# Branch arm widths of the expert products taken from a table by expert

## The chip, the cores and the metric

The kernel runs on one core of one Trainium2 chip. The metric is the device time of one execution in microseconds (us); less is better. The core has five engines that run side by side and wait for each other by semaphores: PE (TensorE, the matrix products), DVE (VectorE), ACT (ScalarE), POOL (GpSimd) and SP (SyncE, which here issues nearly all DMAs). In the profile the weight loads of PE have a row of their own, PEld. An engine's name with a q behind it (PEldq) is its sequencer, which issues the instructions, takes the branches and waits for semaphores.

## What is computed

Three layers follow one another: clustered attention, a mixture of experts with one expert per token, and a gated feed-forward layer. Only the middle one is touched:

```python
def _moe_ref(x, w_gate, w1, w2, capacity):      # x: 1536 tokens x 512; 8 experts, F = 1024, capacity 384
    logits = x @ w_gate
    expert_idx = np.argmax(logits, axis=1)
    ...                                          # gate_w, and disp[e]: the tokens of expert e, at most 384
    h = np.maximum(np.einsum('ecd,edf->ecf', disp, w1), 0.0)
    y = np.einsum('ecf,efd->ecd', h, w2)
    ...                                          # out[i] = gate_w[i] * y[expert of i, place of i]
```

The inputs are drawn from a fixed seed. Worked out with the reference itself, the experts 0 to 7 get 198, 119, 169, 188, 162, 192, 206 and 302 tokens. The kernel doesn't know these counts when it is built; it finds them on the chip.

## The kernel before, in words

The attention runs first, up to about 280 us of the span. Its last part also routes the tokens: each token's row is scattered to a place in DRAM by its expert, and the counts go into registers of all engines. The first 128 tokens of expert 0 are computed ahead, in the attention's tail, so that expert 0 has 198 - 128 = 70 tokens left for the loop that this change touches.

`Experts.run` then goes through the experts 0 to 7 in order. For each expert:

- `l1(mp)`, four times: hidden units, two blocks of 128 each time. The weights stand still in PE (128 x 128 blocks of W1), the tokens of the expert stream past as columns. The result goes to a PSUM tile `hp`.
- `hidden(mp)`: ACT takes the positive part of `hp` into H (high part), DVE subtracts to get the low part.
- `xt`: twelve 128 x 128 transposes on PE bring in the next expert's tokens (PSUM tile `xp`), and ACT and DVE cast them into X.
- `l2(dp)`, twice: the same with H and W2, into PSUM tile `yp`; `result` stores the high and low part into Y, at the expert's offset.

The data is split: each float32 operand is a sum of a high and a low fp32r part, so that a product needs high times high, high times low, and low times high. There are two forms. `both` puts the high and the low part of the tokens side by side in one matmul of 2w columns (line 1207) and follows it with one of w columns for the low weights (line 1208): two matmuls per block of weights, but only as long as 2w fits, that is up to w = 208. Afterwards `products` copies one half out (line 1220, ACT) and adds it (line 1221, DVE). `prod` uses three matmuls of w columns each (line 1199), and no addition.

How many columns w an expert takes is chosen by its count on the chip. `arms` writes every piece of work three times, and each engine branches over the parts that aren't wanted: if the count is over 208, w is 384 (`WIDE`, form `prod`); else if it is over a lower bound, w is 208; else w is that lower bound, which is 128 for expert 0 and 176 for the others. In PE's program the wide arm comes first, then the middle one, then the low one. The branch past the wide arm is line 1185, the one between middle and low line 1188. A branch is made by comparing a register, on each engine's own sequencer.

Weights come from DRAM in eight chunks of 512 KB per expert through a ring of four buffers (`load`, DMAs issued by SP). `split` casts a chunk to its high part on ACT (line 968) and subtracts for the low part on DVE (W1) or POOL (W2, line 969); the next load into a buffer waits for both. The order of all engines is that of the program text (a manual schedule). The feed-forward layer `Glu` follows (lines 1421 and 1439 on PE); its first three weight chunks are converted inside expert 7's work by the hooks (lines 1384 to 1402).

Of the kernel before, what the change touches and what calls it, by code (L numbers as in the profile page):

```python
# [10 lines left out]
F32 = mybir.dt.float32  # L11
# [12 lines left out]
class Attention:  # L24
# [318 lines left out]
    def where(self, g):  # L343
        HJ = self.J // 2
        n, half, r = self.group(g // HJ)
        return 2 * n + r, half * HJ + g % HJ, n, r
# [550 lines left out]
class Experts:  # L897
# [174 lines left out]
    def tail(self, at, go):  # L1072

        nc, rt, KD = self.nc, self.rt, self.KD
        self.room(at)
        a = self.fold(0)
        off = rt.offsets(self.keep[1], at.ps_t.tile([128, 3, 128], F32, tag="t", name="t")[:, 0, 0:self.E])
        next(a)
        yield
        self.rows(0, 0, 1, 2)  # L1080
        nc.gpsimd.memset(rt.gap, 0.0)
        next(a)
        next(a)
        go(4)
        for _ in range(6):
            next(off)
        next(a)
        for i in off:
            end = i
        go(12)  # L1090
        a = self.fold(1)
        rt.after(self.split(0, 7), [end])
        for _ in a:
            pass
        b = self.head2(at)
        for _ in range(16):
            next(b)
        self.cnt0, self.cnt1 = [self.count(1, e, None, rt.CP) for e in range(2)]
        for _ in range(8):
            next(b)  # L1100
        self.px = [at.ps_s.tile([128, 2, 512], F32, tag="s", name="xp") for _ in range(2)]
        for k in range(KD):
            self.turn(0, k)
        with self.tc.If(self.cnt0 > 128):
            for k in range(KD):
                self.turn(1, k)
            with self.tc.If(self.cnt0 > MERGED[-1]):
                for k in range(KD):
                    self.turn(2, k)
        for _ in b:  # L1110
            pass
# [4 lines left out]
    def begin(self):  # L1116

        nc, tc, cnt = self.nc, self.tc, self.cnt0

        def body(w):  # L1120
            for p, a, b in zip(self.px, (0, 2), (2, 4)):
                h, l = [self.X[:, i, a:b, 0:w] for i in range(2)]
                ps = p[:, :, 0:w]
                nc.scalar.copy(out=h, in_=ps)
                nc.vector.tensor_tensor(out=l, in0=ps, in1=h.bitcast(F32), op=ALU.subtract)

        self.arms(cnt, body)
        self.load(8)
        for k in range(self.KD):
            for t in self.Y:  # L1130
                nc.gpsimd.memset(t[:, k, 128:self.rt.N].bitcast(F32), 0.0)
        low = self.settle()
        rt = self.rt
        for f, i in ((lambda: self.rows(1, 0), 0), (lambda: self.load(9), 1), (lambda: self.rows(1, 1), 2),
                     (lambda: self.rows(1, 2), 3)):
            rt.after(f(), [low[i]])
# [21 lines left out]
    def xt(self, e, cnt):  # L1158
        nc = self.nc
        banks = [self.bank("xp") for _ in range(self.KD // 2)]  # L1160

        def turn(t, k):
            return nc.tensor.transpose(banks[k // 2][:, k % 2, t * 128:(t + 1) * 128],  # L1163
                                       self.xr[e][:, t, k * 128:(k + 1) * 128], self.ident)

        def body(w):
            for a, b in ((0, 2), (2, 4)):
                h, l = [self.X[:, i, a:b, 0:w] for i in range(2)]
                ps = banks[a // 2][:, a % 2:a % 2 + b - a, 0:w]
                nc.scalar.copy(out=h, in_=ps)  # L1170
                nc.vector.tensor_tensor(out=l, in0=ps, in1=h.bitcast(F32), op=ALU.subtract)

        for k in range(self.KD):
            for t in range(self.nt):
                turn(t, k)

        with self.tc.If(cnt > MERGED[-1]) as c:
            body(WIDE)
        with c.Else():
            body(MERGED[-1])  # L1180

    def arms(self, cnt, body):

        low = 128 if cnt is self.cnt0 else MERGED[0]
        with self.tc.If(cnt > MERGED[1]) as c:
            body(WIDE)
        with c.Else():
            with self.tc.If(cnt > low) as d:
                body(MERGED[1])
            with d.Else():  # L1190
                body(low)

# [15 lines left out]
            self.nc.tensor.matmul(out[:, 0, 0:w], lhsT=W[1][:, k, cols], rhs=mov[:, 0, k, 0:w], start=False, stop=k == ks - 1)  # L1208

    def view(self, ps, w):  # L1210
        return ps[:, :, 0:w] if w == WIDE else ps.rearrange("p m (a t) -> p m a t", a=2)[:, :, 0, 0:w]

    def products(self, ps, half, W, s, mov, w):

        nc = self.nc
        for m in range(2):
            (self.prod if w == WIDE else self.both)(ps[:, m], W, 2 * s + m, mov, w)
        if w < WIDE:
            t = half[:, :, 0:w]
            nc.scalar.copy(out=t, in_=ps.rearrange("p m (a t) -> p m a t", a=2)[:, :, 1, 0:w])  # L1220
            nc.vector.tensor_tensor(out=self.view(ps, w), in0=self.view(ps, w), in1=t, op=ALU.add)  # L1221
# [17 lines left out]
        nc.vector.tensor_tensor(out=l, in0=v, in1=h.bitcast(F32), op=ALU.subtract)  # L1239

    def half(self):
        return self.p2.tile([128, 2, MERGED[-1]], F32, name="half")

    def l1(self, mp, cnt, last):

        ps, half = self.bank("hp"), self.half()

        def body(w):
            if last is not None:
                self.hidden(mp - 1, last, w)  # L1250
            self.products(ps, half, self.W1, mp, self.X, w)

        self.arms(cnt, body)
        return ps

    def l2(self, dp, cnt, off, final=False):

        ps, half = self.bank("yp"), self.half()
        single = [ps, self.bank("yp")] if final else None

        def body(w):
            if w == WIDE and final:
                for m in range(2):
                    self.prod(single[m][:, m], self.W2, 2 * dp + m, self.H, w)
                    self.result(dp, single[m], off, w, slice(m, m + 1))
                return
            self.products(ps, half, self.W2, dp, self.H, w)
            self.result(dp, ps, off, w)

        self.arms(cnt, body)  # L1270

    def run(self, hook):
        rt, E = self.rt, self.E
        ET = mybir.EngineType
        assert WIDE == rt.CP
        two = [ET.Activation, ET.DVE]
        cnt = self.cnt0
        for e in range(E):
            off = self.count(0, e, two, rt.N)
            then = self.cnt1 if e == 0 else self.count(1, e + 1, None, rt.CP) if e + 1 < E else None  # L1280
            if e == 5:
                rt.hots(self.p1, self.keep[1])
            ps = None
            for mp in range(4):
                if mp == 3:
                    self.arms(cnt, lambda w: self.hidden(2, ps, w))
                ps = self.l1(mp, cnt, ps if mp < 3 else None)
                if mp < 2 and e:
                    self.split(e, 4 + mp)
                if mp and mp < 3 and not e:  # L1290
                    self.split(1, mp - 1)
            if e:
                self.split(e, 6)
            if e == 5:
                rt.tokens(self.bank("xp")[:, 0, 0:2 * rt.B * rt.J])
            self.arms(cnt, lambda w: self.hidden(3, ps, w))
            if e + 1 < E:
                self.xt(e + 1, then)
                self.rows(e + 2, 0)
            if e:  # L1300
                self.split(e, 7)
                self.split(e + 1, 0)
                self.rows(e + 2, 1)
            else:
                for _ in chain(rt.ranks(self.p1), rt.invert(self.p1)):
                    pass
            if e + 1 == E:
                hook(0)
            self.l2(0, cnt, off)
            if e:  # L1310
                self.split(e + 1, 1)
                self.rows(e + 2, 2)
            j = self.split(e + 1, 2)
            if not e:
                rt.after(self.rows(2, 1), [j])
            if e + 1 == E:
                hook(1)
            self.l2(1, cnt, off, e + 1 == E)
            j = self.split(e + 1, 3)
            if not e:  # L1320
                rt.after(self.rows(2, 2), [j])
            cnt = then
        hook(2)
# [152 lines left out]


NRAW = 4
MERGED = [176, 208]
WIDE = 384  # L1480
TINY = 3.4332275390625e-05

# [89 lines left out]
```

## Time and profile before

| what | us |
|---|---|
| median of 3 runs | 766.0 (764.87 to 769.03) |
| the profiled execution, whole | 764.15 |
| its span, first to last instruction | 762.4 |
| PE busy | 743.9 (98% of the span) |
| DVE, ACT, POOL busy | 511.4, 396.9, 280.3 |

The experts' loop takes from 284.9 to 457.3 us of the span; the feed-forward layer takes the rest. A matmul's duration in the profile overlaps the next one's, so the time that one takes on PE is read from the starts of those that follow. In a row of the timeline, "[0.32 <-PE yp L1208]" behind the row says how long the engine was idle before it and what the profile takes to have ended the wait.

### The profile page before, as it was taken

Reading aid. Unit: us, or ns where it says so; the run is one execution under the profiler, and the core shown is the slowest. Engines: PE = TensorE matmul, PEld = TensorE weight load, DVE = VectorE, ACT = ScalarE, POOL = GpSimd, SP = SyncE. Lnnn points to the kernel's source line nnn. Section 1 sums busy time; section 2 is a strip of 40 time slices with the busy share of each in tenths; the row PEclk is TensorE's granted clock in tenths of the full one; section 3 lists DMA queues with packets and bytes.
Section 4 is the critical chain, followed back from the end, with each engine's and each line's share of the span. In section 5 each row is a group of like instructions: output and inputs, shape, how many; then the busy total and the mean of one; then the engine's idle time right before and its main releaser. Section 6 shows DMA issues by size and latency. Waiting matters only on the chain.

```text
span 762.4 us, 12806 instructions
## 1 busy us (share of the span) xinstructions
PE 743.9 (98%) x4334; PEld 622.1 (82%) x4334; DVE 511.4 (67%) x864; ACT 396.9 (52%) x762; POOL 280.3 (37%) x267
## 2 busy tenths in 40 slices
PE   7999999999999999999999999999999999999996
PEld 6777777777776799999899997788888888888885
DVE  4668777688786857667666557777676667677323
ACT  5777686867778655666667534443332222222210
POOL 6120210212216754444684233433333332333245
PEclk9999999999999999999999999999999999999999
DMA  8758869548256346887777632231212211210012
GB/s 195 174 128 211 197 185 255 126 98 187 47 138 204 98 151 186 274 263 246 234 243 231 212 113 83 83 111 56 82 56 60 79 56 56 62 49 1 0 56 110
DMA packets 103789, 102.91 MB, mean 135 GB/s; under 512 B 30896, under 2 KB 90800, under 8 KB 103696
## 3 DMA queue, kind: packets, MB, share of 16 engines
q1 hardware_dynamic: 101632, 95.37, 44.8%
q0 software_dynamic: 1920, 6.29, 2.1%
q8 instruction: 55, 0.90, 0.5%
q14 instruction: 38, 0.31, 0.1%
q10 hardware_dynamic: 144, 0.03, 0.0%
HBM read 68.48 MB, written 12.85 MB: 107 GB/s over the span
## 4 chain that ended last, share of the span: by engine, by line
PE 54%; DVE 3%; ACT 2%; issue 1%; POOL 1%; DMA 1%; ACTq 0%; DVEq 0%; POOLq 0%
PE o L1439 12%; PE g L1421 11%; PE v L1421 11%; PE yp L1207 5%; PE hp L1207 4%; PE hp L1199 2%; PE yp L1199 2%; PE yp L1208 2%; PE hp L1208 2%; PE xp L1163 1%; DVE gtmp L1398 1%; POOL out L1450 1%; DMA raw<-in_moe_w 1%; DVE gtmp L1397 0%; ACT W1h L968 0%
## 5 line engine op out<-in xcount | busy, mean ns | idle before, releaser
L368 DVE TENSOR_REDUCE nm<-s 128x1 f32<-128x768 f32 x96 | 91.1, 949 | 12.8 <-PE s L365 10.5
L969 POOL TENSOR_TENSOR W2l<-raw,W2h 128x1024 fp32r<-128x1024 f32 x29 | 69.2, 2400 | 74.0 <-ACT W2h L968 65.2
L378 ACT ACTIVATE P<-s,nm 128x768 f32<-128x768 f32 x96 | 86.5, 901 | 12.1 <-DVE nm L368 11.7
L397 PE MATMUL t<-ident,P 128*128 128x128 f32 x576 | 81.1, 275 | 0.9 <-ACT PT L400 0.7
L1428 POOL TENSOR_TENSOR ghl<-u,ghh 128x512 fp32r<-128x512 f32 x36 | 50.1, 1391 | 76.2 <-ACT ghh L1427 76.2
L397 PEld LDWEIGHTS t<-ident,P 128*128 128x128 f32 x576 | 68.8, 141 | 7.5 <-DVE PT L402 2.0
L416 PE MATMUL acc<-PT,ldv 128*64 128x384 f32 x384 | 69.3, 495 | 0.1
L1207 PE MATMUL hp<-X,W1h 128*128 128x352 f32 (+2 forms) x224 | 63.4, 358 | 1.1 <-DVE hp L1221 1.1
L1207 PE MATMUL yp<-H,W2h 128*128 128x352 f32 (+2 forms) x224 | 63.7, 359 | 0.8 <-PE yp L1208 0.3
L1447 DVE TENSOR_TENSOR acc<-o,acc 128x512 f32<-128x512 f32 x60 | 41.5, 692 | 33.1 <-PE o L1439 32.9
L365 PE MATMUL s<-Ak,Aq 128*128 128x384 f32 x192 | 58.8, 388 | 4.2 <-ACT P L378 4.1
L1425 DVE TENSOR_TENSOR u<-sg,g 128x512 f32<-128x512 f32 x36 | 24.7, 687 | 54.4 <-ACT sg L1424 51.6
L400 ACT COPY PT<-t 128x384 f32<-128x384 f32 x96 | 45.7, 476 | 27.9 <-PE t L397 27.7
L1427 ACT CAST ghh<-u 128x512 fp32r<-128x512 f32 x36 | 22.4, 622 | 68.2 <-DVE u L1426 68.2
L1208 PE MATMUL yp<-H,W2l 128*128 128x176 f32 (+2 forms) x224 | 55.3, 247 | 0.0
L1208 PE MATMUL hp<-X,W1l 128*128 128x176 f32 (+2 forms) x224 | 55.3, 247 | 0.0
L402 DVE COPY PT<-t 128x384 f32<-128x384 f32 x96 | 52.3, 545 | 1.0 <-PE t L397 1.0
L365 PEld LDWEIGHTS s<-Ak,Aq 128*128 128x128 f32 x192 | 29.4, 192 | 28.3 <-ACT P L378 18.3
L365 PE MATMUL s<-kB,qB 80*128 80x384 f32 (+1 forms) x192 | 50.4, 344 | 0.9 <-DVE qB L294 0.7
L969 DVE TENSOR_TENSOR W1l<-raw,W1h 128x1024 fp32r<-128x1024 f32 x28 | 42.6, 1540 | 12.8 <-ACT W1h L968 12.5
L416 PEld LDWEIGHTS acc<-PT,ldv 128*64 128x64 f32 x384 | 25.1, 136 | 28.1 <-issue 27.2
L176 POOL TENSOR_TENSOR Lk<-Xk,Hk 128x384 fp32r<-128x384 f32 x14 | 14.0, 1001 | 89.9 <-ACT Xk L175 89.9
(301 smaller groups left out, 1952.5 us busy)
## 6 DMA issues: line engine op xcount, KB each, us to landing
raw<-in_moe_w SPq DMA_DIRECT2D x64, 512.0 KB, 4.9
Ak<-Hk SPq DMA_DIRECT2D x32, 192.0 KB, 4.4
moe_rows<-zero SPq DMA_DIRECT2D x8, 768.0 KB, 5.3
xr<-moe_rows SPq DMA_DIRECT2D x24, 256.0 KB, 4.6
raw<-in_moe_w_gate SPq DMA_DIRECT2D x12, 512.0 KB, 3.5
raw<-in_moe_w_val SPq DMA_DIRECT2D x12, 512.0 KB, 3.5
raw<-in_moe_w_out SPq DMA_DIRECT2D x12, 512.0 KB, 3.7
ldq<-in_q SPq DMA_DIRECT2D x16, 192.0 KB, 4.7
```

Of the source, the lines that this page charges most:

```text
L365: nc.tensor.matmul(ps[:, c, 0:HS], lhsT=ql[:, qs], rhs=kr[:, c * HS:(c + 1) * HS], start=a == 0, stop=a == 1)
L368: nc.vector.tensor_reduce(out=nm, in_=ps[:, :, 0:HS], axis=AX.XY, op=ALU.max, negate=True)
L378: nc.scalar.activation(out=P, in_=ps[:, :, 0:HS], func=AF.Exp, bias=nm, accum_out=self.pairs[n]["sum"][:, i, r:r + 1])
L397: nc.tensor.transpose(ps[:, jj, :], P[:, a, jj * 128:(jj + 1) * 128], self.ident)
L402: nc.vector.tensor_copy(PT[:, js, cs], ps)
L416: nc.tensor.matmul(acc[c * D:(c + 1) * D], lhsT=v[:, c * HJ + j], rhs=PT[:, c * HJ + j, :], start=j == 0, stop=j == HJ - 1, tile_position= ...
L969: j = (nc.vector if e and i < 4 else nc.gpsimd).tensor_tensor(out=l, in0=t, in1=h.bitcast(F32), op=ALU.subtract)
L1207: self.nc.tensor.matmul(out[:, :, 0:w], lhsT=W[0][:, k, cols], rhs=mov[:, :, k, 0:w], start=k == 0, stop=False)
L1208: self.nc.tensor.matmul(out[:, 0, 0:w], lhsT=W[1][:, k, cols], rhs=mov[:, 0, k, 0:w], start=False, stop=k == ks - 1)
L1421: nc.tensor.matmul(ps[which], lhsT=W[a], rhs=self.Y[b][:, k, ts], start=k + i == 0, stop=k == KD - 1 and i == 2)
L1428: nc.gpsimd.tensor_tensor(out=hl[:, fc], in0=u, in1=hh[:, fc].bitcast(F32), op=ALU.subtract)
L1439: nc.tensor.matmul(p[t], lhsT=h[a][:, fc, t * 128:(t + 1) * 128], rhs=W[b][:, fc], start=fc == 0 and i == 0, stop=fc == 1 and i == 2)
```

## The change

The three widths no longer are the same for all experts. A table gives each expert its low and its middle width; above the middle one it is 384 as before. Whether an arm uses the form with two matmuls or the one with three now goes by w being over 208, not by w being 384.

```diff
-MERGED = [176, 208]
+MERGED = 208
+ARMS = [(128, 208), (128, 208), (176, 208), (192, 208), (176, 208), (192, 208), (176, 208), (208, 320)]
 WIDE = 384
...
-    def arms(self, cnt, body):
-
-        low = 128 if cnt is self.cnt0 else MERGED[0]
-        with self.tc.If(cnt > MERGED[1]) as c:
+    def arms(self, e, cnt, body):
+
+        low, mid = ARMS[e]
+        with self.tc.If(cnt > mid) as c:
             body(WIDE)
         with c.Else():
             with self.tc.If(cnt > low) as d:
-                body(MERGED[1])
+                body(mid)
             with d.Else():
                 body(low)
...
     def view(self, ps, w):
-        return ps[:, :, 0:w] if w == WIDE else ps.rearrange("p m (a t) -> p m a t", a=2)[:, :, 0, 0:w]
+        return ps[:, :, 0:w] if w > MERGED else ps.rearrange("p m (a t) -> p m a t", a=2)[:, :, 0, 0:w]
...
         for m in range(2):
-            (self.prod if w == WIDE else self.both)(ps[:, m], W, 2 * s + m, mov, w)
-        if w < WIDE:
+            (self.prod if w > MERGED else self.both)(ps[:, m], W, 2 * s + m, mov, w)
+        if w <= MERGED:
...
-            if w == WIDE and final:
+            if w > MERGED and final:
```

The rest of the diff passes the expert's number to `arms`, `l1` and `l2`, and replaces the name `MERGED[-1]` by `MERGED`. The casts of `xt` keep their own two widths, 384 and 208.

## Rows read from the trace of the kernel before

**Rows 1.** The page: busy time and share of each engine; granted clock in 40 slices.
```profile
PE 743.9 (98%) x4334; PEld 622.1 (82%) x4334; DVE 511.4 (67%) x864; ACT 396.9 (52%) x762; POOL 280.3 (37%) x267
PEclk9999999999999999999999999999999999999999
```
**Rows 2.** Line 1207 on PE: duration ns min/median/max, first and last start, forms.
```profile
L1207 PE MATMUL hp<-X,W1h x224: 330/358/404, 284.9 to 412.8; 128*128 128x352 f32 x48, 128*128 128x416 f32 x48, 128*128 128x256 f32 x16
```
**Rows 3.** Timeline of PE where stretches begin: start us, duration us, instruction.
```profile
294.16 0.35 PE L1207 MATMUL yp<-H,W2h 128*128 128x256 f32 x1
301.57 0.38 PE L1207 MATMUL hp<-X,W1h 128*128 128x352 f32 x1
...
321.31 0.39 PE L1207 MATMUL hp<-X,W1h 128*128 128x352 f32 x1
330.09 0.27 PE L1163 MATMUL xp<-ident,xr 128*128 128x128 f32 x1
...
403.53 0.36 PE L1207 MATMUL hp<-X,W1h 128*128 128x416 f32 x1
413.13 0.27 PE L1163 MATMUL xp<-ident,xr 128*128 128x128 f32 x1
...
424.03 0.35 PE L1199 MATMUL hp<-X,W1h 128*128 128x384 f32 x1
440.69 0.34 PE L1199 MATMUL yp<-H,W2h 128*128 128x384 f32 x1
465.67 0.39 PE L1421 MATMUL v<-Yh,W1h 128*128 128x512 f32 x1
468.39 0.39 PE L1421 MATMUL g<-Yh,W1h 128*128 128x512 f32 x1
```
**Rows 4.** Timeline of PE: the idle times inside experts 1 and 4.
```profile
316.87 0.43 PE L1207 MATMUL yp<-H,W2h 128*128 128x352 f32 x1 [0.32 <-PE yp L1208]
368.91 0.40 PE L1207 MATMUL hp<-X,W1h 128*128 128x352 f32 x1 [1.14 <-DVE hp L1221]
372.89 0.40 PE L1207 MATMUL yp<-H,W2h 128*128 128x352 f32 x1 [0.27 <-ACT W2h L968]
```
**Rows 5.** PE's branches, experts 1, 2, 4, 5, 7: ns min/median/max, first and last start.
```profile
L1185 PEldq COMPARE_BRANCH  x1: 2593/2593/2593, 313.9 to 313.9; - x1
L1188 PEldq COMPARE_BRANCH  x8: 208/208/1577, 319.6 to 334.0; - x8
L1188 PEldq COMPARE_BRANCH  x1: 2712/2712/2712, 366.0 to 366.0; - x1
L1188 PEldq COMPARE_BRANCH  x16: 70/123/389, 379.9 to 400.9; - x16
L1185 PEldq COMPARE_BRANCH  x16: 65/120/292, 421.6 to 454.2; - x16
```
**Rows 6.** Instruction DMA of the seven experts from 284 to 421.5 us: packets, MB, share.
```profile
q8 instruction: 26, 0.43, 1.3%
```
**Rows 7.** Stretches: experts 1 and 2, and the feed-forward layer; busy time, clock, DMA share.
```profile
core 0: us, PE busy (x) PEld busy (x) DVE busy (x) ACT busy (x) POOL busy (x), PEclk, DMA share, GB/s
301.50:321.30 19.80, 19.39 (x143) 18.92 (x142) 12.73 (x18) 13.31 (x22) 9.52 (x4) 1.00 0.77 238
321.30:340.10 18.80, 18.80 (x142) 18.80 (x141) 12.91 (x19) 12.97 (x22) 9.48 (x4) 1.00 0.83 259
...
520.00:600.00 80.00, 80.00 (x350) 65.59 (x349) 55.63 (x79) 21.99 (x38) 25.55 (x19) 1.00 0.20 60
```
**Rows 8.** Timeline of ACT and DVE in expert 1: a late weight chunk, the last hidden part.
```profile
308.20 1.05 ACT L968 CAST W2h<-raw 128x1024 fp32r<-128x1024 f32 x1 [1.08 <-DMA raw<-in_moe_w]
312.94 0.52 DVE L1228 SCALAR_TENSOR_TENSOR H<-hp,H 128x352 fp32r<-128x352 f32 x1 [0.75 <-ACT H L1227]
```
**Rows 9.** Timeline of POOL and PE: second feed-forward weight chunk, and its first use.
```profile
454.42 1.30 POOL L1402 TENSOR_TENSOR W1l<-gtmp,W1h 128x512 fp32r<-128x512 f32 x1 [4.99 <-ACT W1h L1401]
458.75 0.47 PE L1421 MATMUL v<-Yh,W1h 128*128 128x512 f32 x1
```

More of the change, by code (lines that the diff above doesn't have):

```diff
@@ L1106, in tail @@
                 self.turn(1, k)
-            with self.tc.If(self.cnt0 > MERGED[-1]):
+            with self.tc.If(self.cnt0 > MERGED):
                 for k in range(KD):
@@ L1125, in body @@
                 nc.vector.tensor_tensor(out=l, in0=ps, in1=h.bitcast(F32), op=ALU.subtract)
-        self.arms(cnt, body)
+        self.arms(0, cnt, body)
         self.load(8)
@@ L1175, in xt @@
                 turn(t, k)
-        with self.tc.If(cnt > MERGED[-1]) as c:
+        with self.tc.If(cnt > MERGED) as c:
             body(WIDE)
         with c.Else():
-            body(MERGED[-1])
-    def arms(self, cnt, body):
-        low = 128 if cnt is self.cnt0 else MERGED[0]
-        with self.tc.If(cnt > MERGED[1]) as c:
+            body(MERGED)
+    def arms(self, e, cnt, body):
+        low, mid = ARMS[e]
+        with self.tc.If(cnt > mid) as c:
             body(WIDE)
@@ L1241, in half, with l1 @@
     def half(self):
-        return self.p2.tile([128, 2, MERGED[-1]], F32, name="half")
-    def l1(self, mp, cnt, last):
+        return self.p2.tile([128, 2, MERGED], F32, name="half")
+    def l1(self, e, mp, cnt, last):
         ps, half = self.bank("hp"), self.half()
@@ L1251, in body, with l2 @@
             self.products(ps, half, self.W1, mp, self.X, w)
-        self.arms(cnt, body)
+        self.arms(e, cnt, body)
         return ps
-    def l2(self, dp, cnt, off, final=False):
+    def l2(self, e, dp, cnt, off, final=False):
         ps, half = self.bank("yp"), self.half()
@@ L1268, in body @@
             self.result(dp, ps, off, w)
-        self.arms(cnt, body)
+        self.arms(e, cnt, body)
     def run(self, hook):
@@ L1274, in run @@
         ET = mybir.EngineType
-        assert WIDE == rt.CP
+        assert WIDE == rt.CP and len(ARMS) == E
         two = [ET.Activation, ET.DVE]
@@ L1285, in run @@
                 if mp == 3:
-                    self.arms(cnt, lambda w: self.hidden(2, ps, w))
-                ps = self.l1(mp, cnt, ps if mp < 3 else None)
+                    self.arms(e, cnt, lambda w: self.hidden(2, ps, w))
+                ps = self.l1(e, mp, cnt, ps if mp < 3 else None)
                 if mp < 2 and e:
@@ L1295, in run @@
                 rt.tokens(self.bank("xp")[:, 0, 0:2 * rt.B * rt.J])
-            self.arms(cnt, lambda w: self.hidden(3, ps, w))
+            self.arms(e, cnt, lambda w: self.hidden(3, ps, w))
             if e + 1 < E:
@@ L1308, in run @@
                 hook(0)
-            self.l2(0, cnt, off)
+            self.l2(e, 0, cnt, off)
             if e:
@@ L1317, in run @@
                 hook(1)
-            self.l2(1, cnt, off, e + 1 == E)
+            self.l2(e, 1, cnt, off, e + 1 == E)
             j = self.split(e + 1, 3)
```

## Prediction

> **What bounds the kernel now.** I read the page first, then PE's timeline through the experts, then the branches of PE's sequencer, then the stretches by expert. PE is busy for 98% of the span and the granted clock is at its upper level, 2.4 GHz, nearly throughout [rows 1]. The experts' loop is no exception: in expert 2, PE is busy for all of 18.8 us while DVE, ACT and POOL are busy for 12.9, 13.0 and 9.5 us [rows 7]. The feed-forward layer behind it is as dense, 80.0 us busy of 80 [rows 7], so what PE saves in the experts the end of the kernel gets, unless something else is late in its place.
>
> **Which arms run.** The forms of line 1207 show them: 16 rows of 256 columns (expert 0, w = 128), 48 of 352 (three experts at 176) and 48 of 416 (three at 208) [rows 2]; expert 7 runs line 1199 with 384 [rows 3]. That agrees with the counts 70, 119, 169, 188, 162, 192, 206, 302 of the document's front. Put into the new table they give: expert 1 goes from 176 to 128, experts 3 and 5 from the middle arm of 208 to the low arm of 192 (192 is not over 192), expert 7 from the wide arm of 384 to a middle arm of 320. Experts 0, 2, 4 and 6 keep their arms.
>
> **What a column costs.** An expert has 32 pairs of matmuls (lines 1207 and 1208) in its first product and 32 in its second. At w = 128, 32 pairs take 301.57 - 294.16 = 7.41 us, 0.2316 a pair; at 176, 330.09 - 321.31 = 8.78 us, 0.2744; at 208, 413.13 - 403.53 = 9.60 us, 0.3000. Single matmuls: 96 of 384 columns take 440.69 - 424.03 = 16.66 us, 0.1735 each; twelve of 512 take 468.39 - 465.67 = 2.72 us, 0.2267 each [all rows 3]. So 128 columns more cost 53.2 ns, 0.416 ns a column.
>
> - *Expert 7, 384 to 320.* 320 columns have no row. By the slope just read, one takes 0.1735 - 64 x 0.000416 = 0.1469 us. 192 matmuls of 0.0266 us less give 5.1 us. The bound on the other side is the slope between the pairs, (0.3000 - 0.2744) / 96 = 0.27 ns a column, which would give 192 x 64 x 0.00027 = 3.3 us. I take 5.1, since the neighbours, 384 and 512, are single matmuls of the same kind as 320; a pair's second matmul is short.
> - *Expert 1, 176 to 128.* 64 pairs x (0.2744 - 0.2316) = 2.7 us, measured at both widths.
> - *Experts 3 and 5, 208 to 192.* A pair then has 576 columns, halfway between 528 and 624: 0.287 us. 64 x 0.013 = 0.8 us each; the lengths read at experts 3 and 5 themselves would give up to 1.1. I take 0.9 each, 1.8 for both.
>
> The sum on PE is 5.1 + 2.7 + 1.8 = 9.6 us. The Trainium skill (TensorE: Matmul & The Clock Gate, "Back-to-back issue gap") gives a single matmul's gap as its columns over 2.4 GHz and a constant. By that formula each column saved would be worth 0.417 ns in the pairs too, and the sum would be about 11.5 us; the trace agrees with it between 384 and 512 columns, and not in the pairs, where 144 columns were worth 42.8 ns.
>
> **What takes some of it back: branches.** PE's sequencer issues ahead of the array. In expert 1 a branch starts at 313.9 us [rows 5]; the product behind it starts at 316.87, after 0.32 us of idle time [rows 4], so PE had work for some 2.6 us more. Most branches take 0.07 to 0.4 us and are hidden. But some take far longer: 2593 ns in expert 1, up to 1577 in expert 2, 2712 in expert 4. In expert 5, which runs the middle arm, none of the line shown is over 389 ns, and in expert 7, in the wide arm, none is over 292 [rows 5]. The long ones come together with instruction DMAs, 26 blocks in seven experts [rows 6], under four an expert. So I read them as jumps into program that has not yet been fetched; low arms, which jump twice in a row over the two others, have them. The Trainium skill (Runtime: NRT & Kernel Launch, "Instruction fetch mechanics") says that a taken branch out of the sequencer's window forces a fetch first. That speaks against putting two more experts on the low arm; the trace agrees for experts 1, 2 and 4.
>
> PE pays what the lead doesn't cover: 0.3 us in expert 1, nothing in expert 2, where it is busy throughout [rows 7], and 1.14 + 0.27 = 1.4 us in expert 4 [rows 4]. The profile names DVE and ACT for these two; I take the first as a branch, because the one of 2712 ns ends at 368.7 [rows 5] and PE goes on at 368.91, and the second with it. The mean of the three experts is 0.6 us. For experts 3 and 5 this is new: 2 x 0.6 = 1.3 us, bounds 0 and 2.8. Their 1.8 shrinks to 0.5. Expert 7's middle arm is now reached by one jump, as in experts 3, 5 and 6, which show no long branch: nothing, at most one stall of 0.5.
>
> **What takes some of it back: weights.** In expert 1 ACT waits 1.08 us for a weight chunk, until 308.20 [rows 8]; nothing before that changes, so the chunk comes no earlier. Behind it, in ACT's order, stand the copies and casts of the remaining hidden blocks, up to the last low part of H on DVE at 312.94 + 0.52 = 313.46 [rows 8]. Narrower operations take perhaps 0.6 us off that chain. The second product needs this part for its seventh block of weights, with 26 of 32 pairs still to come: 312.9 + 26 x 0.2316 = 318.9, against 321.31 now. With the 0.3 us stall of the branch kept, 2.1 us are saved; the lead gets shorter, as the array is faster by a sixth, which adds some 0.4 to the stall. I take 1.7 of the 2.7, with bounds 1.0 and 2.7. Expert 2 then begins earlier with DMA already busy for 0.83 of its time [rows 7]; expert 1 has 0.77 over 19.8 us, which over 18 us would be 0.85. That is still under one, so I cost it at nothing.
>
> **The end of expert 7.** The second converted weight chunk of the feed-forward layer is done at 454.42 + 1.30 = 455.72 and first used at 458.75 [rows 9], 3.0 us of slack. The conversion stands behind the first half of the second product, so it moves with the first 3.8 us of the gain, and its use with 5.1: slack 1.7. Nothing is lost there; if that cover went, the loss would be this difference of 1.3.
>
> **Sum.** 5.1 + 1.7 + 0.5 = 7.3 us. The profiled execution took 764.15 us, 762.4 in the span and 1.75 around it; it becomes 756.9. The median of the runs stands 1.85 above the profiled execution, which I keep: 758.7.
>
> **Rivals.**
> 1. *All of it arrives*: the branches in experts 3 and 5 stay short and expert 1's chain isn't the limit: 766.0 - 9.6 = 756.4. For it: expert 2 hides all its long branches [rows 7]. Against it: experts 1 and 4 [rows 4]. If these lose their stalls of 1.7 us as well, 754.7.
> 2. *Only expert 7 pays*: weights and branches swallow experts 1, 3 and 5 whole: 766.0 - 5.1 = 760.9. For it: the wait at 308.20 and a DMA share of 0.83; against it: no wait of PE for a weight DMA in expert 2.
> 3. *Slower, by instruction fetch*: each of the under four blocks an expert in experts 1, 3 and 5, some 11 in all, stalls PE like the worst wait of expert 4, 1.14 us: 12.5 - 9.6 = 2.9 us more, 768.9; with the whole 2.7 us bare, as little as four of them undo the change and six make it slower by over 0.5%. It decides from nine of the smaller stalls on. Against it: experts 1, 2 and 4 show three idle times in their eleven blocks.
> 4. *The change doesn't do what it says*: a count differs on the chip from the reference's, so that expert 7 stays wide or expert 5 in the middle. With expert 7 wide, 766.0 - 2.2 = 763.8. Against it: all eight arms agree with the counts.
>
> **How the numbers follow.** The forecast has 0.58, rival 1 has 0.18, rival 2 has 0.16, rival 3 has 0.03, rival 4 has 0.05. The likeliest case gives 758.7. The range reaches from rival 1 with some stalls gone, 755.2, to rival 2 with the runs' own spread of about 1.1 us on it, 762.0. About 0.5%, 3.8 us, is what a measurement of this kernel can tell from no change. Forecast and rivals 1 and 2 lie below 762.2, save a little of rival 2: faster 0.91, same 0.06, slower 0.03.
>
> **What would show it.** In the profile after, line 1207 should list 32 rows of 256 columns for hp, 32 of 352, 32 of 384 and 16 of 416, and line 1199 320 columns. Expert 7's first product should last 14.1 us in place of 16.66. Expert 1 should last 18.0 us in place of 19.7 [rows 3], with PE waiting in its second product until about 312.9. Experts 3 and 5 should show branches over 1 us that they don't have now. I am wrong if 320 columns take clearly more than 0.147 us, if PE waits for weight chunks in experts 2 to 6, or if experts 3 and 5 last longer than before.

## The result, and the profile after

The kernel after takes 754.94 us (median of 5 runs, 754.56 to 760.44), the kernel before beside it 765.35: ratio 0.9872, 95% interval 0.9844 to 0.9899, or 9.8 us less by the ratio. Two more sets on other chips give 0.9883 (0.9855 to 0.9910) and 0.9856 (0.9837 to 0.9876). Faster was right; the forecast of 7.3 us less was too small by 2 to 4 us, though the second set's interval still holds it. Applied to the 766.0 of the forecast the ratio gives 756.2, inside the range; the median itself lies 0.3 under the range's lower end.

The page of after, to be read against [rows 1]: span, PE's busy time, granted clock, instruction DMA.

```profile
span 758.7 us, 12766 instructions
PE 736.1 (97%) x4334; PEld 614.3 (81%) x4334; DVE 512.7 (68%) x864; ACT 394.5 (52%) x762; POOL 280.0 (37%) x267
PEclk9999999999999999999989999999999999999999
q8 instruction: 56, 0.92, 0.5%
```

PE has as many instructions as before and 7.8 us less busy time. The one 8 in the clock row belongs to a stall that is told of in the last section; this profiled execution took 760.44 us, the longest of its five.

Lines 1207 and 1199 of after (ns min/median/max, first and last start, forms), against [rows 2]:

```profile
L1207 PE MATMUL hp<-X,W1h x224: 331/357/396, 283.3 to 414.3; 128*128 128x256 f32 x32, 128*128 128x352 f32 x32, 128*128 128x384 f32 x32, 128*128 128x416 f32 x16
L1199 PE MATMUL hp<-X,W1h x64: 307/309/321, 425.5 to 439.3; 128*128 128x320 f32 x64
```

The arms are those that the forecast named: 32 rows of 256 columns, 32 of 352, 32 of 384, 16 of 416, and expert 7 at 320.

PE's timeline in after where stretches begin: experts 1, 2 and 7, expert 7's second product, the feed-forward layer. It answers to [rows 3].

```profile
300.29 0.34 PE L1207 MATMUL hp<-X,W1h 128*128 128x256 f32 x1
...
320.30 0.37 PE L1207 MATMUL hp<-X,W1h 128*128 128x352 f32 x1
...
425.54 0.47 PE L1199 MATMUL hp<-X,W1h 128*128 128x320 f32 x2
...
439.63 0.45 PE L1199 MATMUL yp<-H,W2h 128*128 128x320 f32 x2
...
453.71 0.40 PE L1421 MATMUL g<-Yh,W1h 128*128 128x512 f32 x1
```

Expert 7's first product lasts 439.63 - 425.54 = 14.09 us in place of 16.66, the second 14.08 in place of 16.64. Expert 1 lasts 320.30 - 300.29 = 20.01 us in place of 19.74, with 27% fewer columns than before (128 for 176). The same starts, taken for all experts from the kernel before, from this profile and from a second profile of after (us):

| | e0 | e1 | e2 | e3 | e4 | e5 | e6 | e7 | loop |
|---|---|---|---|---|---|---|---|---|---|
| before | 16.67 | 19.74 | 18.82 | 20.72 | 20.83 | 21.85 | 20.50 | 33.30 | 172.43 |
| after | 16.95 | 20.01 | 19.29 | 19.51 | 18.87 | 27.05 | 20.52 | 28.17 | 170.37 |
| after, second profile | 17.04 | 19.30 | 19.26 | 20.36 | 18.76 | 21.06 | 20.62 | 28.17 | 164.57 |

Three things in it were not in the forecast: expert 1 gains next to nothing, expert 4, which is not changed, gains 2 us, and expert 5 lost 5 us in one profile and not in the other. One profile of expert 1 says little by itself: with 176 columns it lasts 19.1 to 20.6 us in five profiles (mean 19.8), with 128 columns and whole loads 17.5 to 20.0 in eight (mean 19.0), and what it gains expert 2 loses in part. The two together take 38.9 us in the mean of the five and 38.6 in that of the eight.

### The profile page after: what moved, and what is told of

Same layout as the page of the kernel before. It is cut to its first block, busy times and chain, and to the rows that moved or that the text cites. A ratio compares the mean times of both kernels' runs of the same rounds, so it can differ in the third digit from the quotient of the medians.

```text
span 758.7 us, 12766 instructions
## 1 busy us (share of the span) xinstructions
PE 736.1 (97%) x4334; PEld 614.3 (81%) x4334; DVE 512.7 (68%) x864; ACT 394.5 (52%) x762; POOL 280.0 (37%) x267
## 4 chain that ended last, share of the span: by engine, by line
PE 46%; DVE 4%; issue 4%; ACT 3%; DMA 3%; POOL 2%; ACTq 0%; POOLq 0%; DVEq 0%; SPq 0%
PE o L1439 12%; PE g L1421 12%; PE v L1421 11%; DMA raw<-in_moe_w 3%; PE yp L1207 3%; PE hp L1207 2%; PE yp L1199 2%; PE hp L1199 2%; PE yp L1208 1%; POOL rhot L885 1%; PE hp L1208 1%; DVE gtmp L1398 1%; ACT W1h L968 1%; POOL out L1450 1%; DVE gtmp L1397 0%
## 5 line engine op out<-in xcount | busy, mean ns | idle before, releaser
L1207 PE MATMUL yp<-H,W2h 128*128 128x256 f32 (+3 forms) x224 | 65.2, 370 | 3.7 <-DVE H L1228 3.7
L1207 PE MATMUL hp<-X,W1h 128*128 128x256 f32 (+3 forms) x224 | 60.8, 352 | 0.3 <-ACT W2h L968 0.3
L1208 PE MATMUL yp<-H,W2l 128*128 128x128 f32 (+3 forms) x224 | 55.8, 249 | 0.0
L1208 PE MATMUL hp<-X,W1l 128*128 128x128 f32 (+3 forms) x224 | 54.0, 241 | 0.0
L1207 PEld LDWEIGHTS yp<-H,W2h 128*128 128x128 f32 x224 | 44.6, 199 | 4.5 <-issue 3.9
```

Source lines behind the costliest of these rows:

```text
L1207: self.nc.tensor.matmul(out[:, :, 0:w], lhsT=W[0][:, k, cols], rhs=mov[:, :, k, 0:w], start=k == 0, stop=False)
```

## The experiments

Each part of the change alone, and the whole once more; times are of five rounds, against the kernel before on the same chip.

**The whole again.**

> The changed kernel once more, unchanged. In its first profile a DVE instruction of 12 columns (line 893) took 5.66 us, PE then waited 3.36 us in expert 5 and ran at half clock for some 5 us after it. Theory: that is an accident of one execution, not a price of the change: this profile is near 754.5 to 756 us, line 893 takes about 0.17 us, expert 5 lasts about 21.0 us. Rival: the change moves line 893 behind POOL's work for good: the long instruction returns. Both: expert 1 no shorter than 19 us, because its weight chunk lands at 308.

Measured: 0.9883 (0.9855 to 0.9910), 9.0 us less. The long sum of line 893 (told of in the last section) takes 0.65 us here, neither the 0.17 of the theory nor the long form of the rival, and expert 5 takes 21.06; a third profile has the long form again. The profiled execution, 759.19, lies above the expected band all the same: its experts' loop is 5.8 us shorter than that of the first profile, but begins at 287.9 us in place of 283.3, behind an attention that the change doesn't touch.

**Expert 7 alone.**

```diff
 ARMS = [(128, 208), (176, 208), (176, 208), (176, 208),
-        (176, 208), (176, 208), (176, 208), (176, 208)]
+        (176, 208), (176, 208), (176, 208), (208, 320)]
```

> Only expert 7's middle arm of 320 columns; the other widths as before. Theory: 192 matmuls, 64 columns less at 0.416 ns: 5.1 us less, ratio about 0.9933, products of 14.1 us each. Rival with the smaller slope of the pairs: 3.3 us less, ratio 0.9957, 15.0 us each.

Measured: 0.9932 (0.9908 to 0.9957), 5.2 us less. The form of 320 columns in this kernel, the same query as above:

```profile
L1199 PE MATMUL hp<-X,W1h x64: 307/308/323, 426.8 to 440.6; 128*128 128x320 f32 x64
```

The product takes 14.10 us; 96 matmuls in 14.10 us are 0.1469 each.

**Experts 3 and 5 alone**, (192, 208) in their two places of the table.

> Only experts 3 and 5 at 192 columns in the low arm. Theory of columns alone: 1.8 to 2.2 us less, ratio 0.997. Theory of the prediction, with long branches that PE has to wait for: 0.5 us less. In either case the branches of experts 3 and 5 over 1 us are counted.

Measured: 0.9957 (0.9938 to 0.9977), 3.3 us less, where 0.5 was forecast. Expert 3 takes 19.51 us and expert 5 20.89: PE has no wait in either. Expert 4 takes 19.47.

**Expert 1 alone**, (128, 208) in its place.

> Only expert 1 at 128 columns. Theory of the late weight chunk: 0 to 1.7 us less, since the second product waits for work that begins when the chunk lands near 308; ratio 0.998 to 1.000, expert 1 lasts 18 to 20 us. Rival of columns alone: 2.7 us less, ratio 0.9964, expert 1 lasts 17.0 us.

Measured: 0.9996 (0.9975 to 1.0017): no gain that shows. PE's timeline, PE's branches of line 1185 within expert 1 of this kernel (count, ns min/median/max, first and last start), and a stretch of its second product (busy time of PE, PEld, DVE, ACT and POOL with counts, clock, DMA share, GB/s):

```profile
316.34 0.36 PE L1207 MATMUL yp<-H,W2h 128*128 128x256 f32 x1 [1.55 <-DVE H L1228]
```

```profile
L1185 PEldq COMPARE_BRANCH  x9: 208/208/2360, 304.5 to 323.7; - x9
```

```profile
317.90:321.10 3.20, 3.20 (x17) 3.20 (x17) 1.31 (x1) 1.42 (x2) 2.36 (x2) 0.50 0.68 207
```

The first product is shorter by the columns (7.39 us, 8.77 before), the second is longer (10.70, 9.41 before). PE waits 1.55 us in it, until 316.34, by the profile for DVE; DVE there needs a result of ACT, and ACT had waited 1.43 us for a weight chunk, until 314.41. Then the granted clock is 0.50 for 3.2 us, in which PE gets through 17 matmuls, which at the upper level, at 0.2316 a pair, would take 2.0. The wait and these 1.2 us make up the greater part of the 3.3 us that the product takes over the 7.4 of its columns. The branch of 2.36 us begins at 316.6, and PE isn't idle behind it. The three parts alone make 5.2 + 3.3 + 0.3 = 8.8 us, about the whole.

**Why does expert 4 gain? Columns without the path.** Experts 3 and 5 get 192 columns in the middle arm, so that they save the same columns but run the same path through the program as before.

```diff
-ARMS = [..., (176, 208), (176, 208), (176, 208), ...]
+ARMS = [..., (176, 192), (176, 208), (176, 192), ...]
```

> The kernel before, with only the widths of experts 3 and 5 changed, to 176 and 192: the same 16 columns are saved as where these experts take the narrow arm of 192, but here the program's path stays that of the kernel before, the middle arm. Theory (the path of expert 3 decides whether expert 4's branches wait for instructions): expert 4 keeps its long branches on PE (over 1 us each, 20.8 to 21.2 us for the expert), only the columns are gained, 1.8 us, 0.998 of the kernel before; the narrow arm gave 3.3 us. Rival (the columns alone, or the shorter time of expert 3, made expert 4 faster): expert 4 at 18.8 to 19.5 us and 3.3 us gained, as in the narrow arm.

Measured: 0.9984 (0.9960 to 1.0009), 1.2 us less. Expert 3 takes 19.64 us, expert 4 21.89.

**The path without columns.** Expert 3 runs the narrow arm at 206 columns, two fewer than before; all else is as before.

```diff
-ARMS = [..., (176, 208), (176, 208), ...]
+ARMS = [..., (206, 208), (176, 208), ...]
```

> The kernel before, with only expert 3 changed, to 206 and 208: it takes the narrow arm at 206 columns, nearly the 208 of before, so that hardly a column is saved and only the program's path is another. Theory (path of expert 3 decides expert 4's fetch waits): expert 4 falls from 20.8-21.2 us to 18.8-19.5 with no branch over 1.1 us on PE, expert 3 stays at 20.5 to 20.8, and the whole is 1.4 to 2.2 us under the kernel before, 0.997 to 0.998. Rival (saved columns, not the path): expert 4 as before, and the whole within 0.5 us of the kernel before.

Measured: 0.9979 (0.9954 to 1.0003), 1.6 us less. Expert 3 takes 20.51 us, expert 4 18.77. PE's branches within expert 4 (columns as above): lines 1185 and 1188 of after, of the kernel with 192 in the middle arm, and of this one; of before, line 1185, beside the 2712 of [rows 5].

```profile
L1185 PEldq COMPARE_BRANCH  x9: 208/208/417, 358.8 to 377.7; - x9
L1188 PEldq COMPARE_BRANCH  x8: 208/208/790, 359.3 to 376.2; - x8
```

```profile
L1185 PEldq COMPARE_BRANCH  x8: 208/208/3543, 359.5 to 379.7; - x8
L1188 PEldq COMPARE_BRANCH  x8: 70/208/2492, 363.1 to 379.9; - x8
```

```profile
L1185 PEldq COMPARE_BRANCH  x8: 208/208/325, 361.4 to 375.6; - x8
L1188 PEldq COMPARE_BRANCH  x8: 207/208/1050, 361.7 to 375.9; - x8
```

```profile
L1185 PEldq COMPARE_BRANCH  x9: 208/208/2183, 358.8 to 379.7; - x9
```

Expert 4's own code and width are the same in all four. Where expert 3 went through the middle arm, the branch of line 1185 that begins 0.3 us before expert 4 takes 2.2 to 3.5 us; where expert 3 went through the narrow one, at 192 or at 206 columns, it takes 0.42 at most. The same holds in the other profiles: that branch took 1.6 us with expert 7 alone changed and 3.1 with expert 1 alone, both with expert 3 in the middle arm; with expert 3 in the narrow arm no profile shows it. The branch of line 1188 some 5 to 7 us later goes with it: 1.5 to 2.7 us in all four profiles with the middle arm, 0.43 to 0.57 in all ten with the narrow one. Expert 4 lasts 19.2 to 21.9 us in the four profiles of the first kind (mean 20.8), 18.8 to 20.0 in the ten of the second (mean 19.2). So expert 3's path decides about these two branches, and with them about some 1.6 us of expert 4. In time the two halves, 1.2 and 1.6, make 2.8, near the 3.3 of both, but neither interval excludes zero; the separation rests on the profiles.

The traces also show what these branches wait for. In the fourteen profiles PE has 97 branches of more than 0.6 us in the experts' loop, and every one of them ends 1.30 to 1.63 us after a block of instructions (16 KB, queue q8) has landed; of the ordinary ones, of up to 0.25 us, 12% end 1.2 to 1.8 us after one. With expert 3 in the middle arm, the block before the first of expert 4's two branches lands 0.03 to 2.05 us after that branch has begun; in the narrow one, 1.8 to 5.0 us before. In before the block takes from 360.30 to 361.21, and the branch from 360.57 to 362.75; in after the block takes from 356.16 to 357.04, and the branch from 358.84 to 359.25. The instruction queue in before from 360.2 to 360.9 and in after from 355.9 to 356.9 (packets, MB, share):

```profile
q8 instruction: 1, 0.02, 8.1%
```

```profile
q8 instruction: 1, 0.02, 5.5%
```

**Why does expert 1 gain nothing? A weight chunk earlier.** In the first profile of after, PE and ACT wait in the middle of expert 1, between its two products:

```profile
308.77 0.66 PE L1163 MATMUL xp<-ident,xr 128*128 128x128 f32 x4 [0.69 <-DMA xr<-moe_rows]
310.26 0.87 PE L1163 MATMUL xp<-ident,xr 128*128 128x128 f32 x6 [0.83 <-DVE hp L1221]
```

```profile
308.08 1.05 ACT L968 CAST W2h<-raw 128x1024 fp32r<-128x1024 f32 x1 [2.52 <-DMA raw<-in_moe_w]
```

ACT's wait was 1.08 us before [rows 8] and is 2.52 now; but with 176 columns too it is 0.98 to 2.55 in the five profiles, so the difference is not the narrow arm's alone. The chunk's load stands on SP's queue behind the token rows of expert 2.

```diff
-            for n in {8: [10], 9: [11], 10: [12], 11: [13], 12: [14, 15, 16]}...
+            for n in {8: [10], 9: [11], 10: [12, 13], 11: [], 12: [14, 15, 16]}...
```

> The kernel after with one load moved: the chunk of expert 1's weights for which its middle waits is issued on SP one step earlier, ahead of the token rows, instead of behind them. Theory (the 128-column arm nets nothing because the chunk lands late: in the first profile of after ACT waited 2.52 us at 308.08 for it, and the stretch between the first and the second product of expert 1 took 3.6 us against 1.6 before): the wait goes, expert 1 falls from 19.3-20.0 us to 17-18, and the whole to 753-755 us, 1 to 3 us under the kernel after beside it. Rival (the token rows and the gathers hold the middle of expert 1, and the chunk is only the last of several): expert 1 stays within 0.5 us of 19.3 and the whole within 0.7 us of the kernel after.

Measured: 0.9873 (0.9839 to 0.9907), as the kernel after. Expert 1 takes 19.37 us: its middle shrank from 3.6 to 1.25 us, its second product grew from 8.3 or 9.0 to 10.73. That cast waits no more, but the next one does:

```profile
311.44 1.05 ACT L968 CAST W2h<-raw 128x1024 fp32r<-128x1024 f32 x1 [1.03 <-DMA raw<-in_moe_w]
```

Two branches of 2.83 and 2.24 us follow, and PE waits 0.93 and 0.86 us as they end. By its numbers the rival held, but not by its mechanism: the middle did get shorter, and the wait was handed on.

**The same, with line 893 reading PSUM** (why is told in the last section).

```diff
-        nc.vector.scalar_tensor_tensor(out=self.idx, in0=self.toks[:, 0:n], ...
+        nc.vector.scalar_tensor_tensor(out=self.idx, in0=ps[:, 0:n], ...
```

> As the kernel with the early chunk, and the index sum of line 893 reads one of its two inputs from PSUM instead of SBUF, so that DVE doesn't read two SBUF inputs while POOL works through its weight rests. Theory (the 5.66 us that this sum of 128x12 took in the first profile of after, against 0.17 in before, is DVE standing behind POOL's transfers of the shared SBUF access): line 893 takes under 0.3 us in its profile, where it has been 0.17 to 5.66, and the time is that of the early chunk or up to 0.5 us less. Rival (it is a wait by chance for something else): line 893 stays at 0.5 us or more, and the time is that of the early chunk.

Measured: 0.9857 (0.9828 to 0.9887); line 893 takes 0.170 us.

**More weights ahead, and the token rows freed.** On top of both edits, first two more chunks are issued at once, then also the order is dropped that held the token rows back.

```diff
-            ... 10: [12, 13], 11: [], 12: [14, 15, 16]}
+            ... 10: [12, 13], 11: [14, 15], 12: [16]}
```

> The kernel with the early chunk and the index sum that reads PSUM, and two more weight chunks of expert 1 issued on SP as soon as their buffers are free, ahead of the last token rows. Theory (experts 1 and 2 last 19 us whatever their width, because the DMA engines idle at 300 to 304 us, share 0.2 to 0.5, while SP's queue stands, and are then full until 330, so that weights and instructions come late; the early chunk moved one load and only handed the wait to the next ones): with more loads moved into the hole, experts 1 and 2 together lose 0.5 to 2 us against the 38.2 to 38.7 of the three kernels with a 128-column expert 1, and the whole is 753 to 754.5 us. Rival (the two experts are bound by PE and DVE work behind one another, not by arrival): together still 38 to 39 us, and the whole 754.5 to 756.

```diff
-                rt.after(self.rows(2, 1), [j])
+                self.rows(2, 1)
...
-                rt.after(self.rows(2, 2), [j])
+                self.rows(2, 2)
```

> As the kernel with the weights first, and the two loads of token rows of expert 2 that were ordered behind expert 1's weight rests (after the split's last step) are free of that order, so SP's queue doesn't stand behind them from 297 to 303 us. Theory (the hole in the DMA's work is SP's queue standing, and experts 1 and 2 wait for what it delays): DMA share between 300 and 304 us rises from 0.2-0.5 to over 0.7, experts 1 and 2 together fall to 35.5 to 37.5 us, from 38.2 to 38.7, and the whole to 752 to 754 us, 1 to 3 under the kernel after beside it. Rival (the rows in front take the place of the weights that expert 1 needs first): expert 1's first product waits for its weights, the two together 38 us or more, and the whole 754.5 us or more.

Beside them, on the same chip, the kernel after a third time.

> The kernel after, unchanged, on the chip of the two kernels above, as their measure: 754.5 to 756.5 us, experts 1 and 2 together 38.3 to 39.3 us, DMA share of 0.2 to 0.5 for 4 us before the middle of expert 1, and line 893 at 0.2 to 0.8 us, or at several us if POOL's weight rests run back to back beside it.

Measured: weights first 0.9855 (0.9830 to 0.9881), rows freed 0.9847 (0.9825 to 0.9869), after 0.9856 (0.9837 to 0.9876). By the medians the kernel with the rows freed is 2.3 us under after, by the ratios 0.7, and the intervals allow for none as for 2 us or more; so the time doesn't decide, and the profiles have to. Experts 1 and 2 together take 39.31, 38.19 and 37.88 us, where 35.5 to 37.5 was expected with the rows freed. The first of these says little: in that profile a branch of 3.28 us at 299.3, still in expert 0, is followed by a wait of 1.91 us and by a granted clock of 0.50 from 304 to 308. Four-microsecond windows of the third profile of after (busy time of PE, PEld, DVE, ACT and POOL with counts, clock, DMA share, GB/s), and one of the kernel with the rows freed:

```profile
300.00:304.00 4.00, 3.69 (x33) 3.58 (x32) 2.95 (x7) 1.73 (x4) 0.00 (x0) 1.00 0.19 62
304.00:308.00 4.00, 4.00 (x37) 4.00 (x36) 2.45 (x5) 3.26 (x6) 0.91 (x1) 1.00 0.56 174
308.00:312.00 4.00, 4.00 (x38) 3.97 (x37) 1.33 (x4) 1.95 (x5) 2.91 (x2) 1.00 0.93 293
312.00:316.00 4.00, 3.66 (x31) 3.34 (x30) 2.32 (x5) 3.98 (x8) 3.35 (x3) 1.00 0.97 320
```

```profile
300.00:304.00 4.00, 4.00 (x37) 4.00 (x36) 2.68 (x4) 2.68 (x6) 0.00 (x0) 1.00 0.69 226
```

The hole in the DMA's work at 300 us is real, 0.19, and was nearly filled, 0.69 where the theory asked for 0.7. The shorter experts that it asked for didn't come: behind the hole three branches of 2.0 to 2.9 us stand in experts 1 and 2, and the transposes wait 1.12 us for rows. So this theory isn't borne out: none of the three orders of the loads takes the limit away.

**Less to load.** The kernel after, with half of each weight chunk loaded from expert 1's third to expert 2's last. The casts read that half twice, so the engines' work keeps its size; the other half of these weights is left out.

```diff
+        if 10 <= 8 * e + i < 24:
+            return self.nc.sync.dma_start(out=t[:, 0:2], in_=src[:, 0:2])
         return self.nc.sync.dma_start(out=t, in_=src)
...
+        if 10 <= 8 * e + i < 24:
+            t = t[:, 0:2].unsqueeze(1).to_broadcast([128, 2, 2, 256])
+            h, l = [x.rearrange("p (r a) b -> p r a b", r=2) for x in (h, l)]
```

> The kernel after, but of the weight chunks of experts 1 and 2 (from expert 1's third on) only the first half is loaded, 256 of 512 KB each, and the casts and rests read that half twice; the work of PE, ACT, DVE and POOL stays the same in size, and these two experts compute with other weights than the reference's. Theory (what experts 1 and 2 lose, 38 to 39.3 us together against 34.8 of matmuls, is arrival: their weights and their instructions come through DMA engines that are 0.9 to 1.0 busy from 308 to 330 us): DMA share there falls to about 0.6, no branch on PE in expert 1's second half and expert 2's first takes over 1 us, the two together take 34.8 to 36.5 us, and the whole is 2 to 4 us under the kernel after, 751 to 754 us. Rival (a branch to code that isn't there costs its 2 to 3 us however busy the DMA engines are): the weights don't stall any more, but branches of 1.5 to 3.5 us stay, and the two experts take 37 to 38.5 us. Third (PE waits for the chain from DVE to ACT and POOL, not for arrival): 38 us or more with branches under 1 us.

Measured: 0.9865 (0.9833 to 0.9898). The time alone doesn't tell it from after. In the profile experts 1 and 2 take 17.35 + 19.26 = 36.61 us, less than in any of the eight profiles with a 128-column expert 1 and whole loads (37.88 to 39.31, mean 38.55). The two experts as one window (columns as above), first in the third profile of after, then with half the loads:

```profile
303.57:341.45 37.88, 35.95 (x280) 35.10 (x281) 23.78 (x36) 25.35 (x44) 18.98 (x8) 1.00 0.79 249
```

```profile
300.31:336.92 36.61, 35.84 (x283) 35.08 (x282) 24.44 (x36) 25.01 (x44) 18.99 (x8) 1.00 0.60 181
```

The DMA's total in the same two windows:

```profile
DMA packets 8630, 9.45 MB, mean 249 GB/s; under 512 B 321, under 2 KB 7850, under 8 KB 8618
```

```profile
DMA packets 5905, 6.63 MB, mean 181 GB/s; under 512 B 329, under 2 KB 5126, under 8 KB 5894
```

And PE's branches in them (with half the loads the two lines have the numbers 1190 and 1193):

```profile
L1185 PEldq COMPARE_BRANCH  x17: 207/208/1840, 303.7 to 341.2; - x17
L1188 PEldq COMPARE_BRANCH  x16: 207/208/3537, 304.0 to 339.7; - x16
```

```profile
L1190 PEldq COMPARE_BRANCH  x17: 208/208/1605, 300.1 to 336.7; - x17
L1193 PEldq COMPARE_BRANCH  x16: 208/208/870, 300.4 to 335.2; - x16
```

With 2.8 MB less in the way, the same instructions on the same path branch in at most 1.6 us, where the longest took 1.8 to 3.5 in the eight, and no cast waits over 0.53 us for a chunk. The matmuls and transposes alone would be 34.8 us (32 + 32 pairs at 0.2316, as many at 0.2744, and 1.23 twice for the transposes). So of the 3.7 us that the two experts take over that in the mean, about 1.9 are arrival, of weights and of instructions, through busy DMA engines; 1.8 stay unexplained. This is one profile, 0.1 above the expected band, and no gain in time is shown for it, so the exact share stays open.

## Why the prediction was right or wrong

- *Expert 7: right, in place and size.* 5.1 us forecast, 5.2 measured alone; 14.09 us for the product where 14.1 was said. The slope between the neighbours of the same kind (384 and 512, single matmuls) held, the slope between pairs (3.3 us) did not.
- *The end of expert 7: right.* PE goes from the last 320-column matmul to line 1421 at 453.71 without a wait.
- *Columns of experts 3 and 5: right.* 1.8 us forecast; 1.2 in time with the path kept (the interval reaches from a loss of 0.7 to a gain of 3.1), and 1.21 + 0.79 = 2.0 by the second profile's expert 5 and the first one's expert 3.
- *Branches of experts 3 and 5: wrong in sign.* The step said that an expert in the narrow arm pays for jumps of its own, and charged 1.3 us. The long branches that I had read in expert 4 were put down to expert 4's own arm; the first two follow from the arm that expert 3 takes. Expert 3's narrow arm took them away from expert 4 and gave it some 1.6 us. Nor is the middle arm free of them, as the step had read from expert 5 in before: in the four other profiles with expert 5 in that arm, one branch of line 1188 takes 1.4 to 2.6 us. Branches of up to 1.45 us do come in expert 3, as said, but its products last 9.12 and 9.17 us, so PE had work in hand. Instead of 0.5 us the pair of experts is worth 3.3. (The charge itself was also added up wrong: 2 x 0.6 is 1.2, not 1.3.) By the Trainium skill (Runtime: NRT & Kernel Launch, "Instruction fetch mechanics"), a taken branch out of the window must fetch first. The traces agree, as every long branch ends 1.30 to 1.63 us after a block has landed; the runs add that what ran before decides whether the block is there in time. The count of instruction blocks from expert 3 to expert 4 is 8 in before and in after: not fewer fetches, but earlier ones. Why they come later behind the middle arm is not shown.
- *Expert 1: right that weights take some back, wrong in size.* 1.7 us forecast, with a bound of 1.0; measured 0.3 by the ratio, with an interval from a gain of 1.9 to a loss of 1.3, and 0.4 for experts 1 and 2 together by the means of the profiles. The step that failed is the one that set the DMA share of 0.85 against one and costed it at nothing. The mean of 0.77 [rows 7] hid a hole of 0.17 at its start and a full stretch behind, in the kernel before already (windows, columns as above; a packet counts where it starts, so a share can pass one):

```profile
300.00:304.00 4.00, 4.00 (x34) 4.00 (x33) 2.42 (x5) 2.59 (x5) 0.00 (x0) 1.00 0.17 39
308.00:312.00 4.00, 3.91 (x32) 3.70 (x31) 1.74 (x4) 3.02 (x6) 2.59 (x2) 1.00 1.02 306
```

In after a chunk comes 2.5 us late there and a branch takes 2 to 3.5. Nor was the clock in the sum: behind such waits it is at 0.50 in or just before expert 1 for 3 to 7 us, in three of the eight profiles. Pricing one wait and its chain was not enough either: with that chunk early, the next chunk and the branches took its place.
- *The rivals.* By the number, rival 1 (756.4) is the nearest, but not by its mechanism, since expert 1 didn't arrive; its remark that stalls of experts 1 and 4 may go was half right, for expert 4. Rival 2 and rival 3 needed losses by branches in experts 3 and 5, which didn't come; rival 4 is out by the forms.
- *The signs of being wrong.* Expert 5 does last longer than before in two of the three profiles of after, but by the stall of line 893, not by branches.
- *The sum.* Forecast 5.1 + 1.7 + 0.5 = 7.3; measured alone 5.2 + 0.3 + 3.3 = 8.8; together 9.0 to 11.0. One term was 1.4 us too large and another 2.8 too small, so that the whole lands inside the range partly by luck. What is left over the 8.8 lies within the intervals of the parts.

## What to carry to other kernels

Price narrower matmuls from the slope between the nearest rows of the same kind, as this was exact to 0.1 us. Before you count columns saved in a stretch, look at its DMA share in short windows. Here it came near one, and 27% fewer columns gave next to nothing, three other orders of the loads nothing clear of the noise, and half the bytes of the weights 1.9 us in one profile. When branches are long, see when the instruction blocks land, ask which path ran before, and change that on its own before charging the branch to its own code.

## What the runs showed that was not expected

**A small index sum that stops the kernel for 3.4 us.** Expert 5's 27.05 us in the first profile of after come from line 893, a sum of 128 x 12 on DVE that took 0.17 us in before. Beside it POOL works through its weight rests, the subtractions of line 969 that leave the weights' low parts. DVE, POOL and PE in after (timeline; both rows of POOL count the instruction at 389.69), and three stretches of it as windows:

```profile
388.76 5.66 DVE L893 SCALAR_TENSOR_TENSOR idx<-rtoks 128x12 int32<-128x12 f32 x1
385.00 7.09 POOL L969 TENSOR_TENSOR W2l<-raw,W2h 128x1024 fp32r<-128x1024 f32 x3
389.69 4.70 POOL L969 TENSOR_TENSOR W2l<-raw,W2h 128x1024 fp32r<-128x1024 f32 x2
395.03 0.66 PE L1207 MATMUL yp<-H,W2h 128*128 128x384 f32 x1 [3.36 <-DVE H L1228]
```

```profile
389.70:394.90 5.20, 1.98 (x14) 1.72 (x12) 5.20 (x3) 2.53 (x4) 4.69 (x3) 0.87 0.76 234
395.00:400.30 5.30, 5.27 (x20) 5.30 (x21) 2.01 (x3) 0.00 (x0) 0.00 (x0) 0.50 0.75 232
400.30:405.00 4.70, 4.70 (x34) 4.70 (x34) 2.86 (x4) 2.86 (x4) 0.00 (x0) 0.99 0.25 89
```

The sum ends at 394.42, as POOL's run of weight rests ends at 394.39. PE waits 3.36 us and then works 5.3 us at a granted clock of 0.50, the lower level of 1.2 GHz. The third profile of after has the same (5.67 us, PE waits 3.31), the second has not (0.65). These two executions are the longest of their sets, 760.44 and 761.38, but so is the second's, 759.19, without it. The Trainium skill (SBUF — State Buffer, "SBUF: two separate sides") states that a DVE operation with two SBUF inputs and a GpSimd operation that reads SBUF lock each other out of a shared pair of ports, for a whole instruction. The traces agree with it. In the eight profiles in which the sum reads SBUF twice and takes over 0.17 us, it ends 0.03 us after an instruction of POOL. In six of them, 0.34 to 0.95 us, that is the one in which it began, as here with experts 3 and 5 alone (DVE's sum ends at 389.78, POOL's instruction at 389.75):

```profile
389.00 0.78 DVE L893 SCALAR_TENSOR_TENSOR idx<-rtoks 128x12 int32<-128x12 f32 x1
387.38 2.37 POOL L969 TENSOR_TENSOR W2l<-raw,W2h 128x1024 fp32r<-128x1024 f32 x1
```

And with one input from PSUM the sum takes 0.17 us in the midst of such a run of POOL, here in the kernel with the early chunk and that edit:

```profile
390.01 0.17 DVE L893 SCALAR_TENSOR_TENSOR idx<-xp,rtoks 128x12 int32<-128x12 f32 x1
385.91 7.07 POOL L969 TENSOR_TENSOR W2l<-raw,W2h 128x1024 fp32r<-128x1024 f32 x3
390.60 4.74 POOL L969 TENSOR_TENSOR W2l<-raw,W2h 128x1024 fp32r<-128x1024 f32 x2
```

The three kernels with this edit have 0.17 us each, each time in the midst of an instruction of POOL; with two SBUF inputs it took 0.17 to 5.67. In the two long cases it let two ends of POOL's instructions pass before it got in; why, is open, and so is whether the change makes this likelier. A gain is not shown in time: the three ratios, 0.9857, 0.9855 and 0.9847, lie within the interval of after beside the last two, 0.9837 to 0.9876.

**A wait doesn't always cost the clock.** Within the wait of 3.36 us the granted clock fell to 0.50. In the second profile of after, PE was busy for 2.33 of the 4 us from 312, and the clock stayed at 1.00; in the first, busy for 2.29 of the 4 us from 308, it was 0.62 in the mean of the four behind, so that a part of expert 1's 20.01 us is the clock.
